# Decode attention and MLP on one core: one loop of eleven rounds, one joining of all heads, w1 in one transfer

## The chip, the core and the metric

The kernel runs on one core of a Trainium2 chip. The metric is device time in microseconds (us); lower is better. Three runs of the kernel before took 675.19, 675.20 and 675.64 us, median 675.2.

## What is computed

Two tokens (batch of 2) go through an attention over a long cache and through a two-layer MLP; a scalar gate mixes the two results. Everything is 32-bit floating point.

```python
g = sigmoid((x * gate_w).sum(-1))                  # x: 2 x 448
q = x @ wq                                         # 16 heads of 256
p = softmax(q . k_cache / 16)                      # k_cache, v_cache: 2 x 16 x 4096 x 256
a = (p . v_cache) @ wo                             # wo: 4096 x 448
b = relu(x @ w1) @ w2                              # w1: 448 x 1792, w2: 1792 x 448
out = g * a + (1 - g) * b
```

The two caches are 268 MB of the 289.5 MB that are read; each element is used once.

## The kernel before

**Units.** One of the 32 pairs of batch and head is a unit. Its keys and values lie in one row of 16384 floats in each of 128 partitions, 8.39 MB, and are brought by one transfer. Three slots in on-chip memory (`slot0` to `slot2`) take turns. Slot 2 holds wq first, and at the end w1 and w2; slot 0 takes wo at the end.

**The engines' parts in a unit.** TensorE (`scores`, L243) makes the scores in the PSUM tile `ps`, four row groups at a time. VectorE (`values`, L268) takes the negative maximum `nm`, ScalarE (`softmax`, L261) the exponential `prob` and its sum `ls`, and then copies the next unit's query (`pick`, L257). VectorE multiplies each of eight stretches of values by `prob` and sums them into `ov` (L274); after the first it signals `room`, which lets TensorE write `ps` again, and after the last it frees the slot. Each of the three engines has a loop of ten rounds of three units (L283) with addresses from a register. The last two units are written out behind the loop (L326).

**Transfers.** SP issues nearly all of them, in order: wq, units 0 and 1, then one unit whenever a slot comes free (L126 to L133), and `late` (L141): when unit 29's slot is free w1, w1x and w2, and when unit 30's is free wo in five pieces (`CUTS`), each with its own semaphore. The last 448 columns of w1 are not in its transfer. They come as w1x: eight transfers of 8 rows each, into partitions 0 to 63:

```python
for k in range(8):
    o = k // 4 * 4 * 8 + k % 4
    e.dma_start(w1x_sb[o:o + 4 * 7 + 1:4], w1x[k]).then_inc(sem["w1x"], 16)
```

**The start.** x and gate_w come by ScalarE's queue. VectorE spreads x (L176, L178), TensorE makes the gate in two forms (L199, L206), then q in two halves with a bank of PSUM each (L217 to L233). The end of q frees slot 2.

**The joining.** A unit's scores were made in four parts with maxima of their own. `combine` (L294) joins them: transposes of `nm` and `ls`, a common maximum, factors `e4`, the weights `wb` (with the gate), their product with the identity, `os` and the products that bring the heads' outputs into the form `ot`. It runs twice, for units 0 to 15 (after the loop, ahead of the last two units) and for units 16 to 31 (at the end, with wo's products in between).

**The end.** TensorE makes w1's products (L343), the hidden layer is transposed, w2's products (L360) go into `acc`, and wo's (`project`, L372) too, for the first 24 of its 32 blocks. The last eight blocks go into `z` in quarters of the columns. `acc` is copied (L391), folded into `z` by four products with `fold` (L394), and the result is copied and stored. The fold stands ahead of the wait for the last pieces of wo:

```python
t = pr.op(dve, lambda e: e.tensor_copy(a_sb, acc), t)
project(n, CUTS[-3])
for g in range(G):
    mm(z[g * R:(g + 1) * R, :DG], flat(fold), a_sb[:, g * DG:(g + 1) * DG], False, False, t, have_fold)
t = project(CUTS[-3], NO)
```

Of the kernel before, what the change touches and what calls it, by code (L numbers as in the profile page):

```python
# [9 lines left out]
G = 4  # L10
R = P // G
SLOTS = 3
NB = 2
ENGINES = ("tensor", "vector", "scalar", "gpsimd", "sync")


class Program:

    def __init__(self, nc):
        self.nc = nc
        self.code = {e: [] for e in ENGINES}
        self.count = dict.fromkeys(ENGINES, 0)

    def op(self, engine, fn, *after):
        self.count[engine] += 1  # L30
        self.code[engine].append(("op", fn, after))
        return engine, self.count[engine]

    def raw(self, engine, fn, *after):
        self.code[engine].append(("raw", fn, after))

    def loop(self, engine, n, fn):
        self.code[engine].append(("loop", n, fn))

    def emit(self, block, sems):  # L40
        def run(name):
            def body(e):
                seen = {}
                for kind, a, b in self.code[name]:
                    if kind == "loop":
                        with e.Fori(0, a) as i:
                            b(e, i)
                        continue
                    for who, n in b:
                        if seen.get(who, 0) < n:  # L50
                            e.wait_ge(sems[who], n)
                            seen[who] = n
                    if kind == "op":
                        a(e).then_inc(sems[name], 1)
                    else:
                        a(e)
            return body

        for name in ENGINES:
            getattr(block, name)(run(name))  # L60
# [7 lines left out]
def gated_mix_decode(nc, xg, kv, wq, w1, w1x, w2, wo, out):  # L68
# [10 lines left out]
    NF = w2.shape[1] // D  # L79
    DG = D // G  # L80
    FG = NF * P // G
    RB = R // B
    HB = H // NB
    UB = U // NB
    HH = HB // G
    CW = 512
    SCALE = float(DH) ** -0.5
    LOOPS = (U - 2) // SLOTS
    assert U == LOOPS * SLOTS + 2 and SLOTS == 3

# [3 lines left out]
    def bank(name, n=CW):  # L94
        return nc.alloc_psum_tensor(name, [P, n], F32).ap()

    NO = NB * HH * J
    CUTS = (0, NO - 18, NO - 8, NO - 4, NO - 1, NO)
    TAIL = 8
    names = [*ENGINES, "xg", "w1x", "w2", *(f"wo{k}" for k in CUTS[1:]), "query", "score", "top", "prob", "room",  # L100
             *(f"land{s}" for s in range(SLOTS)), *(f"free{s}" for s in range(SLOTS)), "out"]
    sem = {n: nc.alloc_semaphore(n) for n in names}
    land = [sem[f"land{s}"] for s in range(SLOTS)]
    free = [sem[f"free{s}"] for s in range(SLOTS)]
    pr = Program(nc)
    pe, dve, act, pool, sp = ENGINES


    sbuf("gap", P, -(-(-nc.sbuf_base // 32) * 32) % 1024 // 4)
    slot = [sbuf(f"slot{s}", P, LEN) for s in range(SLOTS)]  # L110
    ps = bank("ps", SG)
    pw = [bank(f"pw{k}") for k in range(4)]
    acc = bank("acc")[:, :D]


    def load(s, src, signal, lo=0, hi=None):
        hi = src.shape[1] if hi is None else hi
        return lambda e: e.dma_start(slot[s][:, lo:hi], src[:, lo:hi]).then_inc(signal, 16)  # L118

    xg_sb = sbuf("xg_sb", P, KC, B + 1)  # L120
    pr.raw(act, lambda e: e.dma_start(xg_sb, xg).then_inc(sem["xg"], 16))
    pr.raw(sp, load(2, wq, land[2]))
    for u in range(2):
        pr.raw(sp, load(u, kv[u], land[u]))

    def more(e, i):  # L126
        for k in range(SLOTS):
            s = (2 + k) % SLOTS
            take(e, free[s])
            src = kv[bass.ds(i * SLOTS + (2 + k), 1)].rearrange("o p n -> (o p) n")  # L130
            e.dma_start(slot[s], src).then_inc(land[s], 16)

    pr.loop(sp, LOOPS, more)  # L133

    W1, WX = w1.shape[1], w1x.shape[2]
    w1_sb, w1x_sb = slot[2][:, :W1 + WX], slot[2][:, W1:W1 + WX]
    w2_sb = slot[2][:, W1 + WX:W1 + WX + NF * D]

    def late(e):  # L141
        take(e, free[2])
        load(2, w1, land[2])(e)
        for k in range(8):
            o = k // 4 * 4 * 8 + k % 4
            e.dma_start(w1x_sb[o:o + 4 * 7 + 1:4], w1x[k]).then_inc(sem["w1x"], 16)
        e.dma_start(w2_sb, w2).then_inc(sem["w2"], 16)
        take(e, free[0])
        for lo, hi in zip(CUTS, CUTS[1:]):
            load(0, wo, sem[f"wo{hi}"], lo * D, hi * D)(e)  # L150
        take(e, free[1])

    pr.raw(sp, late)

    ident = sbuf("ident", P, P)

    have_ident = pr.op(pool, lambda e: e.memset(ident, 0.0))
    have_ident = pr.op(pool, lambda e: e.affine_select(
        out=ident, in_=ident, compare_op=ALU.not_equal, fill=1.0, base=0, pattern=[[-1, P]], channel_multiplier=1),
        have_ident)  # L160


    sel = sbuf("sel", P, R)
    t = pr.op(dve, lambda e: e.tensor_reduce(sel, ident.rearrange("p (g r) -> p r g", g=G), axis=AX.X, op=ALU.add),
              have_ident)
    fsum = sbuf("fsum", P, B)
    t = pr.op(dve, lambda e: e.tensor_reduce(fsum, sel.rearrange("p (b r) -> p b r", b=B), axis=AX.X, op=ALU.add), t)
    fold = sbuf("fold", P, B, RB)
    have_fold = pr.op(dve, lambda e: e.tensor_scalar(fold, fsum[:, :, None].to_broadcast([P, B, RB]), 1.0 / RB, None,
                                                     op0=ALU.mult), t)  # L170


    xr = sbuf("xr", P, KC, G, B, RB)
    pr.raw(dve, lambda e: e.wait_ge(sem["xg"], 16))
    for g in range(G):
        pr.op(dve, lambda e, g=g: e.tensor_copy(xr[:, :, g], xg_sb[:, :, :B, None].to_broadcast([P, KC, B, RB])))  # L176
    xu = sbuf("xu", P, KC, UB // B, B)
    have_x = pr.op(dve, lambda e: e.tensor_copy(xu, xg_sb[:, :, None, :B].to_broadcast([P, KC, UB // B, B])))  # L178

    def rows_of(c, i=0):  # L180
        return slice(0, P) if c < KF else slice(i * HP, (i + 1) * HP)

    def flat(a):
        return a.rearrange("p b r -> p (b r)")

    def mm(out, lhs, rhs, start, stop, *after):
        return pr.op(pe, lambda e: e.matmul(out, lhs, rhs, start=start, stop=stop), *after)  # L187

    def transpose(out, src, *after):
        return pr.op(pe, lambda e: e.transpose(out, src, ident), *after)  # L190

    def activate(out, src, fn, *after, **kw):
        return pr.op(act, lambda e: e.activation(out, src, fn, **kw), *after)  # L193


    pr.raw(pe, lambda e: e.wait_ge(sem["xg"], 16))
    for c in range(KC):
        r = rows_of(c)
        t = mm(pw[0][:, :1], xr[r, c].rearrange("p g b r -> p (g b r)"), xg_sb[r, c, B:], c == 0, c == KC - 1, have_x)  # L199
    gp = sbuf("gp", P, 1)  # L200
    gate_read = t = activate(gp, pw[0][:, :1], AF.Sigmoid, t)
    omg = sbuf("omg", P, 1)
    have_omg = pr.op(dve, lambda e: e.tensor_scalar(omg, gp, -1.0, 1.0, op0=ALU.mult, op1=ALU.add), t)
    for c in range(KC):
        r = rows_of(c)
        t = mm(pw[1][:UB, :1], xu[r, c].rearrange("p u b -> p (u b)"), xg_sb[r, c, B:], c == 0, c == KC - 1)  # L206
    gu = sbuf("gu", UB, 1)
    have_gu = activate(gu, pw[1][:UB, :1], AF.Sigmoid, t)


    qt = sbuf("qt", P, T, U)
    W = 2 * KF * DH
    WQ = wq.shape[1] // NB
    wide = sbuf("wide", P, CW)
    pr.raw(pe, lambda e: take(e, land[2], 16))
    busy = [(), ()]
    for i in range(NB):  # L217
        w = slot[2][:, i * WQ:(i + 1) * WQ]
        for c in range(KC):
            for g in range(G):  # L220
                r = rows_of(c, g // 2)
                at = g * W + c * CW if c < KF else G * W + g % 2 * CW
                lhs, rhs = flat(xr[r, c, g]), w[r, at:at + CW]
                last = mm(pw[2 + i][g * R:(g + 1) * R, :], lhs, rhs, c == 0, c == KC - 1)
        t = activate(wide, pw[2 + i], AF.Copy, last, *busy[1], scale=SCALE)
        pt = pw[i]
        for k in range(2 * T):
            t2 = transpose(pt[:, k * P:(k + 1) * P], wide[:, k * P:(k + 1) * P], t, gate_read, have_gu)
        busy[1] = (t2,)
        for s in range(2):  # L230
            dst = qt.rearrange("p t (i g s b) -> p i s t g b", i=NB, g=G, s=2)[:, i, s]
            src = pt[:, ::RB].rearrange("p (s t g b) -> p s t g b", s=2, t=T, g=G)[:, s]
            have_q = activate(dst, src, AF.Copy, t2)  # L233

    nm = sbuf("nm", P, U)
    ls = sbuf("ls", P, U)
    ov = sbuf("ov", P, U, J)
    prob = sbuf("prob", P, SG)  # L240
    query = [sbuf(f"query{s}", P, T) for s in range(SLOTS)]

    def scores(e, u, s):  # L243
        take(e, land[s], 16)
# [222 lines left out]
```

## Time and profile before

| | |
|---|---|
| median of three runs | 675.2 us |
| span of the profiled execution (the profile gives no other time of it) | 674.6 us |
| read from HBM | 289.54 MB, 429 GB/s over the span |
| VectorE busy | 341.5 us (51%) |
| TensorE busy | 224.6 us (33%) |
| ScalarE busy | 59.7 us (9%) |
| mean granted TensorE clock | 0.648 of full speed |

The span runs from the first to the last instruction. In the profile PE is TensorE (PEld its weight loads), DVE is VectorE, ACT is ScalarE, POOL is GpSimd and SP is SyncE; a q behind an engine's name stands for its sequencer. A matrix product of 32-bit numbers shows as two instructions. The mean transfer rate holds the start, where nothing has been requested yet, and the end, so it is lower than the rate of the stretch between them. The share of a busy engine does not say whether it sets the time.

### The profile page before, as it was taken

To read this page: it belongs to the slowest core of one execution; us is meant where nothing else is said; L and a number is where in the kernel's file an instruction comes from. 1 tells how busy PE (TensorE), PEld (TensorE's weight loads), DVE (VectorE), ACT (ScalarE), POOL (GpSimd) and SP (SyncE) were. 2 spreads that over 40 slices of the span, in tenths; PEclk is the share of its full clock that TensorE was granted. 3 is DMA by queue.
4 is the path that set the end of the run, shared out by engine and by line. 5 is a ranking of instruction groups with operands and counts; after the bars stand their busy time and mean duration, and the time that the engine had idled before them with its cause. 6 is when DMAs were issued, how large, how long until landed. Compare 5 with 4: busy or idle time off the path is not lost. (4 is left out here: it accounts for less than half of the span.)

```text
span 674.6 us, 4166 instructions
## 1 busy us (share of the span) xinstructions
PE 224.6 (33%) x1323; PEld 67.0 (10%) x1323; DVE 341.5 (51%) x571; ACT 59.7 (9%) x121; POOL 0.7 (0%) x6
## 2 busy tenths in 40 slices
PE   0643221333332123333322333333222333321277
PEld 0210000001001000100100010010001001000022
DVE  0006566544556664455566545455665544657652
ACT  0020001001000100100010010000001001000010
POOL 0000000000000000000000000000000000000000
PEclk9975567667655666765566676665567666556688
DMA  9999999999999999999999999999999999999997
GB/s 381 428 435 436 436 435 435 435 435 435 435 431 435 435 435 435 435 431 435 435 435 435 435 435 435 435 435 435 435 435 435 435 431 427 435 427 435 400 444 316
DMA packets 6180, 289.66 MB, mean 429 GB/s; under 512 B 992, under 2 KB 1120, under 8 KB 1440
## 3 DMA queue, kind: packets, MB, share of 16 engines
q1 hardware_dynamic: 6032, 289.60, 99.3%
q8 instruction: 3, 0.05, 0.0%
q10 hardware_dynamic: 144, 0.01, 0.0%
q14 instruction: 1, 0.01, 0.0%
HBM read 289.54 MB, written 0.06 MB: 429 GB/s over the span
## 5 line engine op out<-in xcount | busy, mean ns | idle before, releaser
L274 DVE SCALAR_TENSOR_TENSOR slot<-slot,prob 128x1024 f32<-128x1024 f32 x256 | 295.9, 1222 | 65.1 <-DVEq L65 65.1
L251 PE MATMUL ps<-slot,query 128*32 128x512 f32 x1024 | 190.8, 909 | 404.4 <-PEq L65 404.3
L270 DVE TENSOR_REDUCE nm<-ps 128x1024 f32 (+1 forms) x32 | 39.2, 1225 | 230.8 <-DVEq L65 230.8
L251 PEld LDWEIGHTS ps<-slot,query 128*32 128x32 f32 x1024 | 54.7, 158 | 539.1 <-issue 539.0
L263 ACT ACTIVATE prob<-ps,nm 128x1024 f32<-128x1024 f32 x32 | 35.6, 1113 | 385.0 <-ACTq L65 384.9
L263 ACT ACT_TABLE_LOAD x10 | 12.8, 1283 | 163.4 <-ACTq L65 163.4
L274 DVE DVE_READ_ACCUMULATOR slot<-slot,prob (+1 forms) x256 | 21.3, 83 | 0.0
L187 PE MATMUL pw<-slot,xr 128*32 128x512 f32 (+3 forms) x96 | 12.9, 671 | 1.3 <-DMA slot<-in_w1x 1.3
L176 DVE COPY xr<-xg_sb 128x128 f32<-128x128 f32 x4 | 0.6, 224 | 18.0 <-DMA xg_sb<-in_xg 18.0
L187 PE MATMUL pw<-xg_sb,xr 128*128 128x1 f32 (+1 forms) x8 | 1.9, 352 | 21.2 <-DVE xu L178 21.2
L187 PE MATMUL acc<-slot,ot 128*32 128x448 f32 x48 | 7.2, 661 | 2.3 <-DMA slot<-in_wo 2.2
L258 ACT ACTIVATE query<-qt 128x2 f32 (+1 forms) x32 | 6.2, 193 | 0.0
L263 ACT ACTIVATION_READ_ACCUMULATOR prob<-ps,nm (+1 forms) x32 | 6.2, 193 | 0.0
L187 PE MATMUL acc<-slot,hr 128*32 128x448 f32 x28 | 4.9, 810 | 2.0 <-DMA slot<-in_w 2.0
L190 PE MATMUL pw<-ident,nm 128*16 128x128 f32 x2 | 0.7, 328 | 12.6 <-DVEq L324 12.6
L187 PEld LDWEIGHTS pw<-xg_sb,xr 128*128 128x128 f32 (+1 forms) x8 | 1.8, 321 | 21.2 <-DMA xg_sb<-in_xg 21.2
L187 PEld LDWEIGHTS pw<-slot,xr 128*32 128x32 f32 (+1 forms) x96 | 2.8, 122 | 9.9 <-issue 7.7
L190 PE MATMUL pw<-ident,wide 128*128 128x128 f32 x11 | 1.9, 288 | 2.4 <-ACT wide L193 2.4
L310 DVE TENSOR_TENSOR os<-ov,pw 128x128 f32<-128x128 f32 x2 | 0.6, 287 | 4.0 <-PE pw L187 4.0
L318 DVE COPY ot<-pw 128x256 f32<-128x256 f32 x4 | 1.5, 420 | 2.0 <-PE pw L187 2.0
L391 DVE COPY wide<-acc 128x448 f32<-128x448 f32 x1 | 0.6, 624 | 3.1 <-PE pw L187 3.1
L187 PE MATMUL pw<-slot,ot 128*32 128x112 f32 x64 | 2.0, 261 | 0.2 <-DMA slot<-in_wo 0.2
(42 smaller groups left out, 20.9 us busy)
## 6 DMA issues: line engine op xcount, KB each, us to landing
slot<-in_wq SPq DMA_DIRECT2D x1, 7168.0 KB, 19.4
slot<-in_w SPq DMA_DIRECT2D x1, 3136.0 KB, 29.9
slot<-in_wo SPq DMA_DIRECT2D x1, 3136.0 KB, 21.2
slot<-in_w SPq DMA_DIRECT2D x1, 2912.0 KB, 28.2
slot<-in_wo SPq DMA_DIRECT2D x1, 2240.0 KB, 26.1
slot<-in_wo SPq DMA_DIRECT2D x1, 896.0 KB, 27.8
slot<-in_wo SPq DMA_DIRECT2D x1, 672.0 KB, 28.9
slot<-in_kv SPq DMA_DIRECT2D x32, 38.4
```

The costliest lines, as they stand in the source:

```text
L176: pr.op(dve, lambda e, g=g: e.tensor_copy(xr[:, :, g], xg_sb[:, :, :B, None].to_broadcast([P, KC, B, RB])))
L187: return pr.op(pe, lambda e: e.matmul(out, lhs, rhs, start=start, stop=stop), *after)
L190: return pr.op(pe, lambda e: e.transpose(out, src, ident), *after)
L251: m = e.matmul(ps[g * R:(g + 1) * R, c * CW:(c + 1) * CW], query[s][:, t:t + 1].to_broadcast([P, R]), slot[s][:, lo:lo + CW], start=(t == ...
L258: e.activation(query[s], qt[:, :, bass.ds(u, 1)].rearrange("p t o -> p (t o)"), AF.Copy).then_inc(sem["query"], 1)
L263: e.activation(prob, ps, AF.Exp, bias=nm[:, bass.ds(u, 1)], accum_out=ls[:, bass.ds(u, 1)]).then_inc(sem["prob"], 1)
L270: e.tensor_reduce(nm[:, bass.ds(u, 1)], ps, axis=AX.X, op=ALU.max, negate=True).then_inc(sem["top"], 1)
L274: m = e.scalar_tensor_tensor(v, v, 1.0, prob, op0=ALU.mult, op1=ALU.mult, accum_out=ov[:, bass.ds(u, 1), j])
L310: t = pr.op(dve, lambda e: e.tensor_tensor(os, ov[:, us], wp[:, :UB, None].to_broadcast([P, UB, J]), op=ALU.mult), t)
L318: t = pr.op(dve, lambda e, hh=hh: e.tensor_copy(ot[:, i, hh], po[:, hh * B * J:(hh + 1) * B * J].rearrange("p (b j o) -> p j b o", j=J, o= ...
L391: t = pr.op(dve, lambda e: e.tensor_copy(a_sb, acc), t)
```

## The change

The kernel is written anew, with a function for each engine in place of lists of operations. What it computes and the number of bytes stay as they are. The parts:

- **Loop.** TensorE runs all 32 units in one loop of eleven rounds; the third unit of a round stands under a branch that the last round does not take. VectorE's loop runs by unit, and the slot's address comes from a register (`u % SLOTS`). ScalarE keeps ten rounds and two units behind them. There is one `query` buffer instead of three, one semaphore `free` for all slots, and no `room`.
- **Joining.** One joining of all 32 units after the last unit's scores. Its steps for VectorE stand under branches inside the last unit's multiplies (after the fourth and the seventh). The gate is applied where `lhs` (before: `ot`) is written.
- **Last unit.** Its keys and its values come by two transfers, with a semaphore of their own for the values (`late`).
- **w1** comes by one transfer of 128 rows; w1x is gone.
- **wo** comes in six pieces of 14, 6, 4, 4, 3 and 1 blocks; before, five of 14, 10, 4, 3 and 1.
- **Start.** The gate is made from sums by GpSimd and one product; `ident` is made after x has landed; both halves of q use one bank; 1 - g is multiplied into x for the MLP (`xo`) in place of the hidden layer.
- **End.** Waits are instructions of their own that count the semaphore down again (`take`). The four products with `fold` stand behind the wait for the piece of three blocks.

```diff
+    def sync(e):
+        bring(e, slab(2, 0, NQ * WQ), wq, sem["wq"])
+        for u in range(2):
+            bring(e, slot[u], kv[u], land[u])
+        with e.Fori(0, U // SLOTS) as i:
+            for k in range(SLOTS):
+                take(e, sem["free"])
+                s = (k + 2) % SLOTS
+                src = kv[bass.ds(i * SLOTS + (k + 2), 1)].rearrange("o p n -> (o p) n")
+                if k < SLOTS - 1:
+                    bring(e, slot[s], src, land[s])
+                    continue
+                with e.If(i == U // SLOTS - 1):
+                    bring(e, slot[s][:, :T * S], src[:, :T * S], land[s])
+                    bring(e, slot[s][:, T * S:], src[:, T * S:], sem["late"])
+                with e.Else():
+                    bring(e, slot[s], src, land[s])
+        take(e, sem["free"])
+        bring(e, slab(2, 0, W2), w1, sem["w1"])
+        bring(e, slab(2, W2, W2 + NF * D), w2, sem["w2"])
+        take(e, sem["free"])
+        for lo, hi in zip(WO, WO[1:]):
+            bring(e, slab(0, (lo - NF) * D, (hi - NF) * D), wo[:, (lo - NF) * D:(hi - NF) * D], sem[f"wo{hi}"])
...
+    def tensor(e):
...
+        with e.Fori(0, -(-U // SLOTS)) as i:
+            for s in range(SLOTS - 1):
+                scores(s)
+            with e.If(i < U // SLOTS):
+                scores(SLOTS - 1)
+        take(e, sem["query"])
+        e.transpose(tp[:U, :P], nm, ident)
+        e.transpose(tp[:U, P:2 * P], ls, ident).then_inc(sem["tr"], 1)
+        take(e, sem["xo"])
+        take(e, sem["w1"], 16)
+        project(xo, FG, lambda c, g: (g % 2 * W1 + (g // 2 * KF + c if c < KF else 2 * KF) * FG, g // 2))
...
+        for k in range(N - DIRECT, N):
+            if k in WO:
+                e.wait_ge(sem[f"wo{WO[WO.index(k) + 1]}"], 16)
+            if k == N - 4:
+                take(e, sem["a"])
+                for g in range(G):
+                    e.matmul(z[g * R:(g + 1) * R], fold.rearrange("p b r -> p (b r)"), a_sb[:, g * DG:(g + 1) * DG],
+                             start=False, stop=False)
+            for g in range(G):
+                m = e.matmul(z[g * R:(g + 1) * R], lhs[:, k], slab(0, (k - NF) * D + g * DG, (k - NF) * D + (g + 1) * DG),
+                             start=k == N - DIRECT, stop=k == N - 1)
...
+    def vector(e):
...
+        with e.Fori(0, U) as u:
+            take(e, sem["score"], G)
+            e.tensor_reduce(nm[:, bass.ds(u, 1)], ps, axis=AX.X, op=ALU.max, negate=True).then_inc(sem["top"], 1)
+            take(e, sem["prob"])
+            with e.If(u == U - 1):
+                e.wait_ge(sem["late"], 16)
+            for j in range(J):
+                v = ring[:, bass.ds((u % SLOTS) * LEN + (T * S + j * SG), SG)]
+                m = e.scalar_tensor_tensor(v, v, 1.0, prob, op0=ALU.mult, op1=ALU.mult,
+                                           accum_out=ov[:, bass.ds(u, 1), j])
+                if j == 3:
+                    with e.If(u == U - 1):
+                        take(e, sem["tr"])
+                        e.tensor_reduce(nb, mt, axis=AX.X, op=ALU.min).then_inc(sem["nb"], 1)
+                if j == 6:
+                    with e.If(u == U - 1):
+                        take(e, sem["e4"])
...
+            m.then_inc(sem["free"], 1)
```

## Rows read from the trace of the kernel before

**Rows 1.** The page, 40 slices of the span: rate in each, and the bytes.
```profile
GB/s 381 428 435 436 436 435 435 435 435 435 435 431 435 435 435 435 435 431 435 435 435 435 435 435 435 435 435 435 435 435 435 435 431 427 435 427 435 400 444 316
HBM read 289.54 MB, written 0.06 MB: 429 GB/s over the span
```

**Rows 2.** The chain of waits in order of time: start us, us, what.
```profile
642.65 28.93 DMA slot<-in_wo
...
671.63 1.10 PE pw L187 x32
...
672.75 0.27 DVE res L397
```

**Rows 3.** Waits of SP's queue: us in total, times, longest.
```profile
SPq L65 <- SPq L65: 630.0, 34, 33.7
```

**Rows 4.** Transfers by line: count, KB each, median us to landing.
```profile
slot<-in_kv SPq DMA_DIRECT2D x32, 38.4
slot<-in_w1x SPq DMA_DIRECT2D x8, 28.0 KB
```

**Rows 5.** Stretches: us, busy PE, PEld, DVE, ACT, POOL, clock, DMA share, GB/s.
```profile
174.40:232.35 57.95, 17.83 (x96) 5.14 (x96) 31.17 (x52) 5.18 (x10) 0.00 (x0) 0.62 0.99 423
...
580.05:638.00 57.95, 18.93 (x108) 5.12 (x108) 32.34 (x60) 4.15 (x10) 0.00 (x0) 0.62 1.00 435
```

**Rows 6.** Timeline of unit 29: start us, us, engine, line, operation.
```profile
601.80 4.91 PE L251 MATMUL ps<-slot,query 128*32 128x512 f32 x32 [13.28 <-PEq L65]
...
607.06 1.23 DVE L270 TENSOR_REDUCE nm<-ps 128x1024 f32 x1 [6.07 <-DVEq L65]
...
619.28 0.34 SPq L118 DMA_DIRECT2D slot<-in_w  x1
...
619.67 5.48 SPq L146 DMA_DIRECT2D slot<-in_w1x  x8
```

**Rows 7.** Timeline of the start: x there, slot 2 free, unit 1's scores.
```profile
20.34 0.63 DVE L176 COPY xr<-xg_sb 128x128 f32<-128x128 f32 x4 [18.04 <-DMA xg_sb<-in_xg]
...
36.19 0.35 SPq L131 DMA_DIRECT2D slot<-in_kv  x1
...
59.21 6.54 PE L251 MATMUL ps<-slot,query 128*32 128x512 f32 x32 [13.35 <-PEq L65]
```

**Rows 8.** Sequencer instructions of L274, L46, L65: ns min/median/max.
```profile
L274 DVEq FUSED_REGOPS  x240: 57/57/57, 50.3 to 611.2; - x120
...
L46 DVEq COMPARE_BRANCH  x10: 50/56/67, 92.0 to 612.4; - x10
...
L65 PEldq EVENT_SEMAPHORE  x99: 51/51/51, 21.3 to 655.2; - x99
```

**Rows 9.** The page, instruction queue: packets, MB, share of 16 engines.
```profile
q8 instruction: 3, 0.05, 0.0%
```

**Rows 10.** Stretches at the end, columns as in rows 5.
```profile
670.00:670.50 0.50, 0.50 (x21) 0.50 (x23) 0.13 (x1) 0.00 (x0) 0.00 (x0) 1.00 0.62 251
670.50:671.00 0.50, 0.50 (x22) 0.32 (x14) 0.49 (x1) 0.00 (x0) 0.00 (x0) 1.00 0.64 247
671.00:671.50 0.50, 0.44 (x10) 0.16 (x8) 0.00 (x0) 0.00 (x0) 0.00 (x0) 1.00 0.22 82
671.50:672.00 0.50, 0.37 (x16) 0.37 (x20) 0.00 (x0) 0.00 (x0) 0.00 (x0) 1.00 0.04 14
```

**Rows 11.** Timeline of TensorE at the end: w1, w2, wo, fold.
```profile
648.07 3.35 PE L187 MATMUL pw<-slot,xr 128*32 128x448 f32 x32 [1.29 <-DMA slot<-in_w1x]
...
655.12 4.90 PE L187 MATMUL acc<-slot,hr 128*32 128x448 f32 x28 [1.96 <-DMA slot<-in_w]
...
662.53 1.72 PE L187 MATMUL acc<-slot,ot 128*32 128x448 f32 x8 [2.19 <-DMA slot<-in_wo]
...
666.10 4.19 PE L187 MATMUL acc<-slot,ot 128*32 128x448 f32 x32
...
671.04 0.40 PE L187 MATMUL pw<-wide,fold 128*32 128x112 f32 x8
```

More of the change, by code (lines that the diff above doesn't have):

```diff
@@ L12 @@
 SLOTS = 3
[L13 to L60, printed above, removed]
+CW = 512
+DIRECT = 8
 def take(e, sem, n=1):
@@ L65, in take, with settle, gated_mix_decode @@
     e.sem_inc(sem, -n)
-def gated_mix_decode(nc, xg, kv, wq, w1, w1x, w2, wo, out):
+def settle(e, sem, op):
+    op.then_inc(sem, 1)
+    take(e, sem)
+def gated_mix_decode(nc, xg, kv, wq, w1, w2, wo, out):
     U, _, LEN = kv.shape
@@ L95, in bank @@
         return nc.alloc_psum_tensor(name, [P, n], F32).ap()
[L97 to L101, printed above, removed]
+    WO = [NF]
+    for n in (14, 6, 4, 4, 3, 1):
+        WO.append(WO[-1] + n)
+    assert WO[-1] == N
+    names = ["xg", "wq", "w1", "w2", *(f"wo{k}" for k in WO[1:]), *(f"land{s}" for s in range(SLOTS)), "late",
+             "pool", "vec", "act", "const", "fold", "sums", "gate", "omg", "xo", "proj", "wide", "pt", "hr",
+             "query", "score", "top", "prob", "free", "tr", "nb", "e4", "wb", "wp", "os", "po", "ot",
+             "acc", "a", "z", "res", "out"]
@@ L120, in gated_mix_decode @@
-    xg_sb = sbuf("xg_sb", P, KC, B + 1)
[L121 to L133, printed above, removed]
@@ L137, in gated_mix_decode @@
[L137 to L151, printed above, removed]
@@ L153, in gated_mix_decode @@
-    pr.raw(sp, late)
+    ring = sbuf("ring", P, SLOTS * LEN)
+    slot = [ring[:, s * LEN:(s + 1) * LEN] for s in range(SLOTS)]
+    xg_sb = sbuf("xg_sb", P, KC, B + 1)
     ident = sbuf("ident", P, P)
[L157 to L160, printed above, removed]
+    ones = sbuf("ones", P, P)
     sel = sbuf("sel", P, R)
-    t = pr.op(dve, lambda e: e.tensor_reduce(sel, ident.rearrange("p (g r) -> p r g", g=G), axis=AX.X, op=ALU.add),
-              have_ident)
@@ L177, in gated_mix_decode @@
[L177 to L213, printed above, removed]
-    wide = sbuf("wide", P, CW)
[L215 to L233, printed above, removed]
@@ L239, in gated_mix_decode @@
     ov = sbuf("ov", P, U, J)
[L240 to L244, printed above, removed]
-        take(e, sem["query"])
-        take(e, sem["room"])
-        for c in range(SG // CW):
-            for t in range(T):
-                for g in range(G):
-                    lo = t * S + g * SG + c * CW
-                    m = e.matmul(ps[g * R:(g + 1) * R, c * CW:(c + 1) * CW],
-                                 query[s][:, t:t + 1].to_broadcast([P, R]), slot[s][:, lo:lo + CW],
-                                 start=(t == 0), stop=(t == T - 1))
-                    if c == SG // CW - 1 and t == T - 1:
-                        m.then_inc(sem["score"], 1)
@@ L323, in gated_mix_decode @@
-    have_ot = []
-    for _ in combine(0, pr.op(dve, lambda e: e.drain())):
-        pass
-    for u in range(LOOPS * SLOTS, U):
-        for e, f in stages.items():
-            more = (u + 1 < U,) if e == act else ()
-            pr.raw(e, lambda e_, f=f, u=u, more=more: f(e_, u, u % SLOTS, *more))
-    done = pr.op(dve, lambda e: e.drain())
-    hs = wide[:, :FG]
-    hr = sbuf("hr", P, NF, R)
-    ph, pt = pw[3], pw[2]
-    pr.raw(pe, lambda e: (take(e, land[2], 16), e.wait_ge(sem["w1x"], 16 * 8)))
@@ new lines, in gated_mix_decode, with slab @@
+    wb = sbuf("wb", U, G, R)
+    os = sbuf("os", P, U, J)
+    lhs = sbuf("lhs", P, N, R)
+    a_sb = wide[:, :D]
+    res = sbuf("res", P, DG)
+    ps = bank("ps", SG)
+    ph, pt, po, tp = (bank(n) for n in ("ph", "pt", "po", "tp"))
+    acc = bank("acc")[:, :D]
+    z = bank("z")[:, :DG]
+    mt, lt, wp, gp = tp[:U, 0:P:R], tp[:U, P:2 * P:R], tp[:, 2 * P:2 * P + U], tp[:, 3 * P:3 * P + B]
+    W2 = 2 * W1
+    def slab(s, lo, hi, rows=slice(0, P)):
+        return ring[rows, s * LEN + lo:s * LEN + hi]
```

324 lines of the change are left out of this document (171 added, 153 removed).

## The prediction

> **What bounds the kernel now.** I read the page's transfer rate first. Apart from the first slice and the last three the queues move 427 to 436 GB/s in every slice, and 289.54 MB at 435 GB/s are 665.6 us of the span's 674.6 [rows 1]. The chain of waits says the same of the end: its last 33 us are 28.9 us of landing wo, then 1.1 us of TensorE and 0.27 us of VectorE [rows 2]; the store closes the span. The third view is the waits of SP, which issues nearly all transfers: 34 waits, 630.0 us together, all for a slot to come free [rows 3]. That looks like a queue kept waiting, and is not: a unit's transfer lands 38.4 us after its issue [rows 4], while 8.39 MB at 434 GB/s take 19.3 us, so at every issue another unit's 19 us are still ahead. The transfers are the bound; an engine counts only before the first transfer, after the last, or where it delays an issue by more than 19 us.
>
> The profile gives no other time of its execution than the span, 674.6 us. The median of the three runs is 675.2, so I put 0.6 us around the span and carry it through. About 0.2% (1.35 us) is what a measurement of this kernel can tell from no change.
>
> **The change part by part.**
>
> *The loop of eleven rounds, VectorE by unit, branches.* Unit 29 shows the period: scores at 601.80, maximum at 607.06, slot free before 619.28 [rows 6]. VectorE is taken for 12.2 us of 19.3, so 7 us a unit are spare, and 19 us of latency before the queue would run dry. The new loop adds register operations for the slot's address and three branches a unit. One register operation took 57 ns and one branch 56 ns, and both ran under the multiplies of 1.22 us [rows 8]. From nothing (all hidden) up to three operations for each of 8 multiplies and three branches, all exposed: 8 x 3 x 0.057 + 3 x 0.056 = 1.5 us. Both ends lie inside the 7 us: I take 0. The one `query` buffer and the dropped `room` add no wait: the next query is written after the exponential has read `ps`. SP's new branch costs 0.05 to 0.1 us ahead of an issue with 19 us of cover: 0.
>
> *The start.* The gate now goes through GpSimd, `ident` is made after x has landed, and the two halves of q share one bank, so they run strictly in turn. x is there at 20.34, slot 2 is free at 36.19, and unit 1 is there at 59.21 [rows 7]. Slot 2's next load has to be issued before about 58. From x to the free slot it is 16 us now; GpSimd's steps and the serial halves add between 0 and half of that again, 8 us; cover 22 us, taken as 0. Unit 0's scores may start about 1 us later, which 19 us of cover hide too.
>
> *One joining of all heads.* The first half's joining stood between units 29 and 30 and delayed only unit 30; it goes, for nothing, because wo, which waits for that slot, is queued about 14 us (w1 and w2) ahead of its turn. The last unit's keys now land 9.6 us before its values, so its maximum and exponential are done when the values land. From about 641: eight multiplies 9.2 us, up to 2 us for the pieces in between, then the joining's last steps, 3 us: about 655. wo's first piece is waited for until 662.53 [rows 11]. So it is hidden, with 7 us of cover.
>
> *w1 in one transfer of 128 rows.* Its issue falls from nine transfers to one, 5.5 us of SP [rows 6]. That was hidden, since unit 31 was still coming: 0. What counts is where the bytes go. w1x moves 8 x 28.0 KB [rows 4] in transfers of 8 rows; the others have 128. The engines do not end together: the share of the 16 that is busy is 0.62 from 670.0, 0.64 from 670.5, 0.22 from 671.0 and 0.04 from 671.5 [rows 10]. That is about six done at 670, eight more by 671, and two or three late until 671.6, the landing that the chain ends with [rows 2]. One engine moves 434/16 = 27.1 GB/s; 229 KB over eight engines are 1.06 us each, just the step between the six and the eight. I read the eight as w1x's engines, and the late ones as two of the other eight. Spread over sixteen, w1x's share is 0.53 us for each: the eight end 0.53 us sooner, the late ones 0.53 us later. If the late ones are of the eight it is -0.53. I take +0.53, since otherwise the middle step would not hold eight.
>
> [...]
>
> *The order at the end.* Before, the four folding products (eight instructions, 0.40 us) ran at 671.04, ahead of the wait for wo's next to last piece [rows 11]; the last 32 instructions then took 1.10 us from its landing [rows 2]. In the new code the wait comes first and the products stand behind it, with the last four k's queued behind them. At 1.10/32 = 0.034 us each, eight are 0.27 us; the bounds are 0.27 and the whole 0.40. I take 0.27. The waits are instructions of their own now; one took 51 ns on TensorE [rows 8]; two on the path, 0.1 us, between 0 and 0.2. The cut of wo into six pieces and of unit 31 into two adds no bytes; I put it at 0, within 0.1 either way.
>
> *Code.* Three instruction fetches of 0.05 MB in all ran beside the transfers [rows 9]: 16 KB at 27.1 GB/s is 0.6 us of one engine, and whoever serves it stays behind. With two units' scores no longer unrolled, one fetch can go, or move to another engine. Bounds -0.6 and +0.6; I take -0.1.
>
> Sum: 0.53 + 0.27 + 0.1 - 0.1 = +0.8 us. Span 675.4, time **676.0 us**. Bounds: -0.53 + 0.27 + 0 - 0.6 - 0.1 = -1.0 and 0.53 + 0.40 + 0.2 + 0.6 + 0.1 = +1.8.
>
> **The rivals.**
>
> *The balance goes the other way, or the late engines are gone.* Then -0.53 or less replaces +0.53: 675.2 - 0.53 + 0.27 + 0.1 - 0.1 = 674.9. For it: the windows name no engine. Against it: the step of eight.
>
> *TensorE falls behind at the end (slower).* Before, unit 31's scores ended shortly before w1's products, which took 3.35 us for 32 at full clock [rows 11]. Now TensorE idles about ten us before them, and work after an idle stretch starts at the low clock: unit 1's 32 took 6.54 us [rows 7]. w1 would end 3 us later, w2 about 662 instead of 660. From wo's first piece 48 instructions remain up to the copy of `acc`: at the fast 4.19/32 = 0.131 us they are 6.3 us, at the slow 1.72/8 = 0.215 us 10.3 us [rows 11]. Add 1.1 us for the next four k's. From 662.5 that is 669.9 or 673.9, and the landing that matters is about 672.1. It decides once TensorE needs over 9.6 us here, that is if it stays slow for nearly all 48; the price is then 1.8 us and about 1 us for the last 40 instructions: 678.8. Against it: before, the slow stretch lasted 3 us and the 32 that followed were fast.
>
> *Branches bring code in again.* Ten rounds' backward branches cost no fetch before: three in the whole span [rows 9]. Were each of eleven rounds to fetch 16 KB on one engine, 11 x 0.6 = 6.6 us: 682. [...]
>
> *The queue loses less (faster).* The stretch 174 to 232 moved 423 GB/s where the last full one moved 435 [rows 5]: 1.6 us. Did that not recur, with 674.9 besides, 673.3. Nothing in the change touches it, as far as I see.
>
> **How the numbers follow.** Forecast 0.70 (676.0, its own range 675.2 to 676.9); balance the other way 0.13 (674.9); TensorE behind 0.09 (678.8); code fetched again 0.03 (682); queue loses less 0.05 (673.3). The range 674.6 to 677.2 takes in the first two with nearly all bounds and leaves out the rest, 0.17. Slower by over 0.2% is above 676.55: a fifth of the forecast, 0.14, with 0.12 of the slow rivals: 0.26. Faster, below 673.85: 0.05. Within: 0.69.
>
> **What would show it.** The share of busy engines in the last 3 us should fall in one large step and leave two or three late ones, later by 0.5 us than before; a last landing earlier than before's refutes the w1 term. The eight folding instructions should stand behind the wait for wo's next to last piece, with about 1.4 us from there to the end of TensorE. Unit transfers should still be 38 us from issue to landing; much less means that the queue ran dry and the first part is wrong. More instruction packets than the three would speak for the code rival; a granted clock near 0.5 from 663 to 669, with the copy of `acc` after the last landing, for TensorE.

## The result and the profile after

The changed kernel takes 676.68 us (median of 21 runs, 676.33 to 678.21) beside 675.64 us (21 runs, 675.19 to 676.71) for the kernel before: a ratio of 1.0014, 95% interval 1.0008 to 1.0021, so 0.5 to 1.4 us longer. The forecast was 676.0 us and +0.8 us. The profiled execution has a span of 675.3 us, 0.7 more than before's.

The page after, in the lines that answer to [rows 1], [rows 4] and [rows 9] (the last two from its list of transfers and of DMA queues):

```profile
GB/s 381 427 436 435 435 435 435 435 435 435 435 435 435 435 435 435 435 435 435 435 435 435 435 435 435 435 435 435 435 435 435 435 435 435 435 435 425 426 434 282
...
q8 instruction: 3, 0.05, 0.0%
...
HBM read 289.54 MB, written 0.06 MB: 429 GB/s over the span
...
ring<-in_kv SPq DMA_DIRECT2D x31, 38.7
```

The transfers still set the pace: the same bytes, 435 GB/s in the middle, 38.7 us from a unit's issue to its landing. Three instruction packets of 16 KB and one of 8 KB, as before. What differs is the end. The stretches of 57.95 us and of the last microseconds after (us; busy PE, PEld, DVE, ACT, POOL; clock; DMA share; GB/s), to be held against [rows 5] and [rows 10]:

```profile
174.40:232.35 57.95, 17.36 (x96) 4.39 (x96) 31.40 (x52) 5.18 (x10) 0.00 (x0) 0.65 1.00 434
...
669.50:670.00 0.50, 0.34 (x16) 0.35 (x20) 0.36 (x1) 0.00 (x0) 0.00 (x0) 1.00 0.57 219
670.00:670.50 0.50, 0.50 (x28) 0.39 (x17) 0.26 (x1) 0.00 (x0) 0.00 (x0) 1.00 0.16 65
670.50:671.00 0.50, 0.13 (x8) 0.00 (x0) 0.00 (x0) 0.00 (x0) 0.00 (x0) 1.00 0.11 43
671.00:671.50 0.50, 0.15 (x8) 0.18 (x12) 0.00 (x0) 0.00 (x0) 0.00 (x0) 1.00 0.07 25
671.50:672.00 0.50, 0.50 (x28) 0.50 (x25) 0.00 (x0) 0.00 (x0) 0.00 (x0) 1.00 0.00 0
```

The first row is the stretch whose rate I had put down as a rival: before's profile shows 423 GB/s there, this one 434. I had read too much into it. These views count a packet whole where it starts. A unit's packets are 65.5 KB, and 16 of them are under way at once (at 100, 300 and 500 us of both traces), so about 1 MB can fall to either side of an edge, which is 18 GB/s over 57.95 us. In the last full stretch, 580.05 to 638.00, it is the other way round: 435 before [rows 5], 425 after. Over all the full stretches together both profiles moved the same (before, then after):

```profile
58.50:638.00 579.50, 180.54 (x972) 52.49 (x972) 314.09 (x515) 50.72 (x100) 0.00 (x0) 0.62 1.00 433
```

```profile
58.50:638.00 579.50, 178.04 (x992) 44.91 (x992) 314.98 (x513) 50.49 (x99) 0.00 (x0) 0.64 1.00 433
```

With each packet of the trace shared out over its own time, before is 0.32 MB behind after from 232 us on, which is 0.7 us and not 1.6. A later kernel (eight drains, further down) is as far behind from 290 us on. So executions differ by this much on the way, and two profiles can't be subtracted as they are. The other rows show the new shape of the end: where before had two steps (0.62 and 0.64, then 0.22), the share falls from 0.57 to 0.16 at once. After's trace has 16 increments of a semaphore for the landing of wo's next to last piece: 14 of them come by 670.03 us, and two late ones at 670.78 and 671.21.

The end itself, timeline after (start us, us, engine, line, operation), beside [rows 11] and [rows 2]:

```profile
646.99 4.95 PE L174 MATMUL ph<-ring,xo 128*32 128x448 f32 x32 [5.69 <-PEq L19]
...
655.02 3.20 PE L230 MATMUL acc<-ring,lhs 128*32 128x448 f32 x28
...
662.21 7.24 PE L230 MATMUL acc<-ring,lhs 128*32 128x448 f32 x48 [3.98 <-DMA ring<-in_wo]
...
671.35 0.40 PE L238 MATMUL z<-wide,fold 128*32 128x112 f32 x8 [0.72 <-PEq L19]
671.54 0.97 PE L241 MATMUL z<-ring,lhs 128*32 128x112 f32 x32
673.09 0.28 DVE L326 COPY res<-z 128x112 f32<-128x112 f32 x1 [2.83 <-DVEq L19]
673.39 0.35 SPq L111 DMA_DIRECT2D out<-res  x1
```

w2's products are over at 658.2, wo's first piece is waited for (idle 3.98 us), so the joining is hidden. The folding products now start behind the landing. And the last product ends at 671.54 + 0.97 = 672.51, but the copy starts at 673.09: 0.58 us. Before's timeline has the same 32 products from 671.63, for 0.97 as well, to 672.60, and the copy at 672.75: 0.15 us.

```profile
671.63 0.97 PE L187 MATMUL pw<-slot,ot 128*32 128x112 f32 x32 [0.19 <-DMA slot<-in_wo]
672.75 0.27 DVE L397 COPY res<-pw 128x112 f32<-128x112 f32 x1 [1.76 <-PE pw L187]
```

The chain of waits puts 0.48 us of after's down to "issue", that is to no wait that the profile knows, where before's has 0.02 between its two pieces ([rows 2]: 671.63 + 1.10 = 672.73 to 672.75):

```profile
672.60 0.48 issue
673.09 0.28 DVE res L326
```

Nothing in my sum had half a microsecond there.

### The profile page after: what moved, and what is told of

Read it like the earlier page. It is cut to its first block, busy times and chain, and to the rows that moved or that the text cites. A ratio compares the mean times of both kernels' runs of the same rounds, so it can differ in the third digit from the quotient of the medians.

```text
span 675.3 us, 4348 instructions
## 1 busy us (share of the span) xinstructions
PE 214.3 (32%) x1297; PEld 56.7 (8%) x1297; DVE 339.1 (50%) x556; ACT 59.2 (9%) x119; POOL 2.2 (0%) x14
## 5 line engine op out<-in xcount | busy, mean ns | idle before, releaser
L301 DVE SCALAR_TENSOR_TENSOR ring<-ring,prob 128x1024 f32 x256 | 296.0, 1221 | 77.3 <-DVEq L19 77.3
L189 PE MATMUL ps<-ring,query 128*32 128x512 f32 x1024 | 183.0, 880 | 415.1 <-PEq L19 415.1
L295 DVE TENSOR_REDUCE nm<-ps 128x1024 f32 x32 | 39.2, 1225 | 213.9 <-DVEq L19 213.9
L189 PEld LDWEIGHTS ps<-ring,query 128*32 128x32 f32 x1024 | 46.2, 154 | 551.2 <-issue 551.2
L301 DVE DVE_READ_ACCUMULATOR ring<-ring,prob x256 | 21.2, 83 | 0.0
L230 PE MATMUL acc<-ring,lhs 128*32 128x448 f32 x76 | 10.4, 688 | 4.0 <-DMA ring<-in_wo 4.0
L174 PE MATMUL ph<-ring,xr 128*32 128x512 f32 (+1 forms) x64 | 9.9, 759 | 1.7 <-PEq L19 1.7
L174 PE MATMUL ph<-ring,xo 128*32 128x448 f32 (+1 forms) x32 | 5.0, 766 | 5.7 <-PEq L19 5.7
L230 PEld LDWEIGHTS acc<-ring,lhs 128*32 128x32 f32 x76 | 3.0, 134 | 10.8 <-issue 5.9
L174 PEld LDWEIGHTS ph<-ring,xr 128*32 128x32 f32 (+1 forms) x64 | 2.1, 129 | 7.9 <-issue 7.9
## 6 DMA issues: line engine op xcount, KB each, us to landing
ring<-in_kv SPq DMA_DIRECT2D x2, 4096.0 KB, 33.9
ring<-in_kv SPq DMA_DIRECT2D x31, 38.7
```

What stands on the lines that cost most here:

```text
L174: m = e.matmul(ph[g * R:(g + 1) * R, :width], x[r, c], slab(2, at, at + width, r), start=c == 0, stop=c == KC - 1)
L189: m = e.matmul(ps[g * R:(g + 1) * R, c * CW:(c + 1) * CW], query[:, t:t + 1].to_broadcast([P, R]), slot[s][:, at:at + CW], start=t == 0, s ...
L230: m = e.matmul(acc[g * R:(g + 1) * R], lhs[:, k], w, start=k < G, stop=k >= N - DIRECT - G)
L295: e.tensor_reduce(nm[:, bass.ds(u, 1)], ps, axis=AX.X, op=ALU.max, negate=True).then_inc(sem["top"], 1)
L301: m = e.scalar_tensor_tensor(v, v, 1.0, prob, op0=ALU.mult, op1=ALU.mult, accum_out=ov[:, bass.ds(u, 1), j])
```

## The experiments

My theory: the change costs what the last microseconds cost, by terms that add (w1's balance, the order of the folding products, the last wait). The rivals: the terms are not what holds the end (TensorE, VectorE or the joining is), or the half microsecond is something else than the wait. The interval of one comparison is about 0.6 us to either side, so a single term of 0.3 to 0.5 us is read from the trace, and the times judge the sums.

Beside the times I give the median span of all executions of a kernel (21 of the changed kernel: 675.3 us; 11 or 12 of each variant; 101 of the kernel before beside the experiments: 674.3). The two can disagree, because a time is longer than its span: by 1.3 to 1.45 us in the executions of the two kernels, but by 1.7 to 2.0 us in some of the variants of the changed one (six of 11 with the last wait in the copy, nine of 11 with three parts taken back, two of 11 with two). In the three profiled executions among these the trace has an 8 KB instruction packet 1.6 to 1.7 us behind the span's end; no other profile has one there.

**w1 whole in the kernel before.**

```diff
-        for k in range(8):
-            o = k // 4 * 4 * 8 + k % 4
-            e.dma_start(w1x_sb[o:o + 4 * 7 + 1:4], w1x[k]).then_inc(sem["w1x"], 16)
...
```

(Left out: w1's one transfer takes in these columns, and TensorE's wait for `w1x` goes.)

> The kernel before with only w1 changed to one transfer of 128 rows. My theory (w1x's eight transfers kept eight engines 1.06 us busier, and the late ones are two of the other eight): the middle step in the share of busy engines goes, most end together near the old mean, the late ones end about 0.5 us later; time of before plus 0.5 us. Rival 1 (the late ones are of w1x's eight): minus 0.5 us. Rival 2 (split or whole is all the same): 0, and the middle step stays.

675.65 us, ratio to before 0.9998 (0.9989 to 1.0007). The stretches at the end:

```profile
670.00:670.50 0.50, 0.50 (x24) 0.50 (x20) 0.12 (x1) 0.00 (x0) 0.00 (x0) 1.00 0.25 100
670.50:671.00 0.50, 0.50 (x20) 0.33 (x10) 0.50 (x1) 0.00 (x0) 0.00 (x0) 1.00 0.17 68
671.00:671.50 0.50, 0.50 (x14) 0.22 (x16) 0.00 (x1) 0.00 (x0) 0.00 (x0) 1.00 0.13 50
```

The middle step is gone, as the theory has it, and shares of 0.25 to 0.13 are left, two to four of the 16 engines. That these end 0.5 us later was not seen: the last products start at 671.44 here, at 671.63 in before's profile.

```profile
671.44 0.97 PE L184 MATMUL pw<-slot,ot 128*32 128x112 f32 x32
```

Nor does the time show it: its interval, -0.7 to +0.5 us, holds 0 and ends just short of 0.53, and the median span is before's, 674.3 us.

**w1x back in the changed kernel.**

```diff
-        bring(e, slab(2, 0, W2), w1, sem["w1"])
+        bring(e, slab(2, 0, W2 - WX), w1, sem["w1"])
+        for k in range(8):
+            o = k // 4 * 4 * 8 + k % 4
+            bring(e, slab(2, W2 - WX, W2, slice(o, o + 4 * 7 + 1, 4)), w1x[k], sem["w1x"])
...
```

(Left out: TensorE's wait for `w1x` and the addresses of its columns.)

> The changed kernel with w1x's eight transfers put back, nothing else. My theory: six engines end first, eight about 1 us later, the late ones about 0.5 us earlier than without w1x; the whole 0.5 us shorter than the changed kernel, so about 0.5 us above before. Rival 1: 0.5 us longer than the changed kernel. Rival 2: the same as the changed kernel.

676.82 us, ratio 1.0018 (1.0009 to 1.0027). In the profiled execution the folding products start at 670.81 instead of 671.35, and its span is 674.6 us instead of 675.3.

```profile
670.81 0.40 PE L243 MATMUL z<-wide,fold 128*32 128x112 f32 x8 [0.72 <-PEq L19]
```

But this is the shortest of the 11 executions; their median span is 675.4, no shorter than the changed kernel's. So the run fits my theory in its trace, and the second rival in its times and spans; more on this further down.

**Folding products ahead of the wait.** (The same two statements, `if k == N - 4` before `if k in WO`.)

> The changed kernel with the four folding products ahead of the wait for wo's next to last piece. My theory: from that piece's landing to the last product 1.1 us instead of 1.4, the whole 0.27 us shorter than the changed kernel. Rival (TensorE is not what the last copy waits for, or the copy of acc comes late): 0, with the folding products still after the landing.

676.65 us, ratio 1.0008 (0.9999 to 1.0017), span of the profiled execution 675.3, median 675.0. The timeline:

```profile
670.71 0.38 PE L236 MATMUL z<-wide,fold 128*32 128x112 f32 x8
671.50 0.97 PE L241 MATMUL z<-ring,lhs 128*32 128x112 f32 x32 [0.41 <-DMA ring<-in_wo]
673.06 0.27 DVE L326 COPY res<-z 128x112 f32<-128x112 f32 x1 [3.53 <-DVEq L19]
```

The products moved ahead of the landing, and from the landing to the last product it is 0.97 us now, while after's products from 671.35 to 672.51 take 1.16 and themselves begin behind the landing: about 0.2 us. But in this execution the landing came 0.15 us later, and the 0.6 us ahead of the copy stayed. The time alone can't show the term; the median span is 0.3 us below the changed kernel's.

**The last wait carried by the copy.**

```diff
-        take(e, sem["z"])
+        e.wait_ge(sem["z"], 1)
         e.tensor_copy(res, z).then_inc(sem["res"], 1)
```

> The changed kernel with VectorE's last wait (for z) carried by the copy itself instead of an instruction that also counts the semaphore down. In the changed kernel 0.5 us passed between that wait's end and the copy, 0.1 us in other places with the same pair. Theory A (the pair of instructions costs it): the copy starts within 0.1 us of the last product, 0.4 us shorter. Theory B (something else holds VectorE at this point, as the code fetch that starts at the same time): the gap stays, within 0.1 us the same.

676.26 us, ratio 1.0007 (0.9998 to 1.0016), span of the profiled execution 674.8, median 674.7:

```profile
671.59 0.98 PE L241 MATMUL z<-ring,lhs 128*32 128x112 f32 x32
672.62 0.27 DVE L326 COPY res<-z 128x112 f32<-128x112 f32 x1 [2.50 <-PE z L241]
```

From the last product (672.57) to the copy 0.05 us instead of 0.58, 0.4 us less in time and 0.6 us less in the median span. It speaks for the pair of instructions; the next three took that apart.

**The wait apart, in the kernel before.**

```diff
-    t = project(CUTS[-3], NO)
+    t0 = project(CUTS[-3], NO)
     res = sbuf("res", P, DG)
-    t = pr.op(dve, lambda e: e.tensor_copy(res, z[:, :DG]), t)
+    pr.raw(dve, lambda e: (e.wait_ge(sem[pe], t0[1]), e.sem_inc(sem["room"], 1)))
+    t = pr.op(dve, lambda e: e.tensor_copy(res, z[:, :DG]))
```

> The kernel before with VectorE's last wait (ahead of the copy of the result) as an instruction of its own. Theory A (an instruction apart costs 0.5 us at this place): the copy starts 0.5 us after the last product and the time of before rises by 0.45 us. Theory B (it costs 0.1 us as elsewhere, and the gap of the changed kernel has to do with its code): 0.1 us.

675.70 us, ratio 1.0004 (0.9995 to 1.0013). The timeline at its end:

```profile
670.92 0.97 PE L187 MATMUL pw<-slot,ot 128*32 128x112 f32 x32
672.15 0.28 DVE L398 COPY res<-pw 128x112 f32<-128x112 f32 x1 [1.82 <-PE pw L187]
```

The last product ends at 671.89, the copy starts at 672.15: 0.26 us, 0.1 more than before's 0.15. A wait apart costs 0.1 us here, not 0.5, so the pair of instructions alone isn't the cause. (The wait's instruction counts another semaphore up here, not its own down; the next run has the very pair.)

**Eight drains at the head of VectorE's program** (`for _ in range(8): e.drain()`), the wait left as it is in the changed kernel.

> The changed kernel with eight drain instructions at the head of VectorE's program, where it waits anyway; the last wait stays an instruction of its own. Theory A (the 0.5 us between that wait and the last copy come from where the copy stands in VectorE's code): the copy starts 0.1 us after the wait, 0.4 us shorter than the changed kernel, about 676.3. Theory B (the pair of instructions costs 0.5 us here wherever it stands; the four reductions of the other run did something else): the gap stays at 0.5.

676.30 us, ratio 1.0007 (0.9998 to 1.0016). First the end of this run's timeline, then that of the changed kernel with 16 unused products on TensorE (two experiments on), which left VectorE's program alone:

```profile
672.18 0.98 PE L241 MATMUL z<-ring,lhs 128*32 128x112 f32 x32
673.33 0.28 DVE L328 COPY res<-z 128x112 f32<-128x112 f32 x1 [1.99 <-DVEq L19]
```

```profile
671.87 0.97 PE L243 MATMUL z<-ring,lhs 128*32 128x112 f32 x32
673.42 0.28 DVE L328 COPY res<-z 128x112 f32<-128x112 f32 x1 [2.47 <-DVEq L19]
```

673.16 to 673.33 is 0.17 us, 672.84 to 673.42 is 0.58. The same pair of instructions costs 0.1 or 0.5 us according to where it stands in VectorE's program.

The sequencer's rows of the traces, which the timeline leaves out, show what the place does. From the end of the wait to the copy 0.49 us pass in the changed kernel and in the three variants with the gap, 0.09 in the three without. Those 0.40 us have not gone in the run with eight drains. They stand eight VectorE instructions earlier, between the last multiply's read of the accumulator and the next wait, where 0.55 us pass instead of 0.14. With the last unit in one transfer, which makes VectorE's program shorter, they stand two instructions later, behind the copy and its drain (0.46 us instead of 0.05). So in these kernels VectorE's sequencer stops once for 0.40 us at one place of its code, and this shows ahead of the last copy only where that place lies behind the last wait. The reason stays open. What the traces show beside it is an instruction packet of 8 KB: it starts 1.1 to 1.2 us after the stop begins in the five kernels that have the stop in the last 3 us (after: 672.60 and 673.76). That the two belong together is not shown. With the wait carried by the copy no stop is seen behind the last product.

**Four more reductions a unit on VectorE.**

```diff
                 if j == 3:
+                    with e.If(u < U - 1):
+                        for x in range(4):
+                            e.tensor_reduce(extra[:, bass.ds(u, 1), x], prob, axis=AX.X, op=ALU.max)
```

> The changed kernel with four reductions of 128x1024 more on VectorE in each unit but the last (results unused), about 4.5 us of 19.3 more. My theory (7 us a unit are spare, the transfers set the pace): the same time within 0.2 us, units still 38 us from issue to landing. Rival (VectorE's unit is near the pace): each unit is longer by what passes 19.3 us; 1 us a unit would be 30 us in all.

676.49 us, ratio 1.0012 (1.0003 to 1.0021), 0.2 below the changed kernel. Groups of instructions (count, busy us, mean ns) and the unit's transfer:

```profile
L307 DVE TENSOR_REDUCE extra<-prob 128x1024 f32 x124 | 142.4, 1210 | 0.0
...
L296 DVE TENSOR_REDUCE nm<-ps 128x1024 f32 x32 | 39.2, 1224 | 79.0 <-DVEq L19 79.0
```

```profile
ring<-in_kv SPq DMA_DIRECT2D x31, 33.9
```

142 us more of VectorE, none of it in the time. Slots come free later, so a transfer is issued 4.8 us later and waits that much less in the queue: 33.9 us to landing instead of 38.7, still far over one unit's 19.3. (The shift of VectorE's program also closed the half microsecond at the end: the copy starts at 672.82, 0.17 us after the last product. The 0.2 us less in time are no gain of the reductions.)

**16 unused products on TensorE** ahead of w1's.

```diff
+        for _ in range(16):
+            e.matmul(z, ident, ones[:, :DG], start=True, stop=True)
         take(e, sem["xo"])
```

> The changed kernel with 16 unused products on TensorE between the last unit's transposes and w1's products, so that it doesn't idle there. My theory (the low clock of w1's products is hidden by the wait for w2 and wo): w1's 32 instructions take about 3.4 us instead of 4.95, the granted clock in that stretch is 1.0, and the time is the same within 0.2 us. Rival (TensorE behind sets the end): shorter by what w1's products gain, 1 us or more.

676.88 us, ratio 1.0017 (1.0008 to 1.0026).

```profile
641.76 5.04 PE L209 MATMUL z<-ones,ident 128*128 128x112 f32 x32
...
647.27 3.35 PE L174 MATMUL ph<-ring,xo 128*32 128x448 f32 x32 [0.47 <-PEq L19]
...
662.53 7.60 PE L232 MATMUL acc<-ring,lhs 128*32 128x448 f32 x48 [3.00 <-DMA ring<-in_wo]
```

w1's products fell from 4.95 us, after 5.69 us of idling and at a mean granted clock of 0.67, to 3.35 us, which is what the kernel before took for them at a granted clock of 1.00. The time didn't fall: the gain goes into the wait for wo. TensorE doesn't set the end here.

**The last unit in one transfer** (the branch in SP's loop and the wait for `late` taken out).

> The changed kernel with the last unit's keys and values in one transfer. My theory (the joining is hidden by 7 us now; without the split the last unit's chain starts 9.7 us later, less about 2 us of maximum and exponential that ran behind unit 30): ot about 661, wo's products start about 1 to 2 us late, time 0 to 0.5 us longer. Rival 1 (all heads' joining is hidden anyhow): 0, wo's first products still wait for their transfer. Rival 2 (the joining sets the end as soon as the split goes): 2 us or more longer.

676.70 us, ratio 1.0010 (1.0001 to 1.0019).

```profile
658.75 0.38 PE L208 MATMUL tp<-ident,wb 32*128 32x32 f32 x2 [2.46 <-PEq L19]
...
660.98 9.89 PE L223 MATMUL acc<-ring,lhs 128*32 128x448 f32 x74
...
671.40 0.62 DVE L315 COPY wide<-acc 128x448 f32<-128x448 f32 x1 [8.88 <-DVEq L19]
672.12 0.40 PE L231 MATMUL z<-wide,fold 128*32 128x112 f32 x8
672.31 0.98 PE L234 MATMUL z<-ring,lhs 128*32 128x112 f32 x32
```

wo's products now trail: `acc` is copied at 671.40 instead of 669.64, and the folding products wait for it until 672.12 (after: 671.35). That is 0.8 us later. VectorE's program got shorter by the wait and a branch, the half microsecond before the last copy went (673.29 to 673.46), and so the time is level with the changed kernel and 0.4 us above the one with the shifted program, the fair partner (in median spans 675.3 and 674.9). So the joining of all heads is hidden only because of the split; with it TensorE still waits 3.98 us for wo's first piece.

**Parts taken back together.** The folding products and the last wait (two), and w1x as well (three):

> The changed kernel with the folding products ahead of the wait and the last wait carried by the copy, w1 still in one transfer. My theory (the terms add): 0.27 and 0.45 us below the changed kernel, about 676.0, and 0.3 to 0.5 us above the kernel that has w1x's eight transfers as well (675.67). Rival (w1's transfer costs nothing in time): level with that kernel and with before.

> The changed kernel with three parts taken back at once: w1x's eight transfers, the folding products ahead of the wait, the last wait carried by the copy. My theory: the terms add, -0.5 (last landing), -0.27 (products) and -0.45 (copy) against the changed kernel: span 674.1, time 675.5 us, level with before. Rival (the lost time lies elsewhere, as in the code fetch beside the store or in what follows the span): at most half of it comes back, 676.1 or more.

Two: 675.84 us, ratio 1.0002 (0.9993 to 1.0011), span of the profiled execution 674.3, median 674.4. Three: 675.67 us, ratio 1.0001 (0.9992 to 1.0010), span 673.8, median 674.0. Ends of their chains of waits, two first:

```profile
671.35 1.02 PE z L241 x32
672.36 0.02 issue
672.39 0.27 DVE res L326
```

```profile
670.79 1.02 PE z L246 x32
671.81 0.02 issue
671.83 0.28 DVE res L331
```

Both are level with before, so the order of the products and the wait are most of what the change cost, by the medians 0.84 us (676.68 to 675.84) of 1.04. This is clear of the noise: the 11 executions with two parts lie between 675.33 and 676.44 us, the changed kernel's 21 between 676.33 and 678.21.

The two kernels differ in w1x alone, and in both the last products wait for wo's next to last piece: it is there 0.56 us earlier with w1x. The other profiles bear this out, the one with the last unit in one transfer left out, where the folding products wait for `acc`. The products behind that piece start at 670.79 to 671.63 us in the five profiles with w1x (median 670.92) and at 671.35 to 671.99 in the eight without (median 671.46): 0.54 us. That is the size and the sign of my term in the landing.

Between the times of the two kernels it is 0.17 us, between their median spans 0.4, and with w1x back in the changed kernel, or w1 whole in the one before, it is nothing. The spans say why that can be. Of before's 101, 55 lie at 673.8 to 674.4 us, 40 at 674.9 to 676.2 and 6 between; with w1 whole all 11 lie between 674.0 and 674.9. So w1x seems to end the transfers earlier in some executions and later in others, as it would if the late engines were sometimes of the eight that I read as its own and sometimes not, the two cases of my forecast. The traces name no engine, and none of the five with w1x is from the upper end of its kernel's spans, so this isn't shown.

**64 drains at the head of TensorE's program**, on the kernel with three parts taken back.

> As the kernel with three parts taken back, and 64 drain instructions at the head of TensorE's program, where it waits for x anyway. Theory A (TensorE's code is fetched in blocks ahead of need, and the third block's fetch falls into the end because of where the code stands): all fetches come 64 instructions earlier, the last one at or before 667 instead of 672, and the store's last landing follows its issue by 1.55 us instead of 1.85; 0.3 us shorter than without the drains. Theory B (the fetch has nothing to do with TensorE's place in its code): fetches and store as without the drains.

675.60 us, ratio 1.0003 (0.9994 to 1.0012), span 674.1. Store: 1.6 us from issue to landing with and without the drains, so the 0.3 us to be gained wasn't there. In the changed kernel it took 1.9:

```profile
out<-res SPq DMA_DIRECT2D x1, 56.0 KB, 1.9
```

Across the kernels it is 1.6 to 1.9 us, with and without instruction packets in the stretch ahead of it. What makes the difference I couldn't settle. Of the three 16 KB packets the middle one came 9 us earlier with the drains (650.88 instead of 659.84 us) and the others did not (43.73 and 670.86 instead of 43.67 and 670.71), so neither theory holds as it stands.

## Why the prediction was right, point by point

- **The bound, and that nothing on the way counts.** Right. 142 us more of VectorE cost nothing, the start hides in its cover (slot 2's next load was issued at 37.47 us instead of 36.19), and w1's products are hidden at a granted clock of 0.67.
- **w1 in one transfer, +0.53 us.** Right in the traces: the step comes and goes with w1x (shares of 0.62 and 0.64 before, 0.55 and 0.54 with three parts taken back), and the products behind the landing that counts start 0.54 us later without it, between the medians of the profiles. Of that landing's 16 increments five come by 669.76 us before, eight from 670.64 to 670.97 and three from 671.30 to 671.59; after, thirteen come from 669.31 to 669.72. That the eight are w1x's engines was my reading; no trace names an engine. The last of these increments came 0.4 us earlier after than before, which I had named as a refutation. By this single pair the term failed. The test was too weak for it: before's profile was 0.7 us behind on the way, and its landing is the latest of the five with w1x. In the times the term isn't shown: 0.17 us between the pair, nothing in the other two comparisons.
- **Folding products, +0.27 us.** Their place behind the landing and about 0.2 us show in the trace, 0.3 us in the median spans. In the times it shows only together with the wait (from 676.26 to 675.84 us).
- **Waits as instructions of their own, +0.1 us within 0 to 0.2.** This term was mis-sized. One of them cost 0.5 us at the end of VectorE's program, because the stop of 0.40 us fell just behind it; carried by the copy it is gone from the trace, and the time is 0.4 us shorter (less than one comparison can tell by itself). Elsewhere it is the 0.1 that I had taken.
- **Code, -0.1 us.** As many packets as before; no gain. A 16 KB packet took 0.95 to 0.97 us in the profiles before and after, not the 0.6 of my sum. That whoever serves it stays behind was an estimate, and no trace names the engine. The landings fit it: in the profile after, one of the 16 increments of the last unit's values comes 0.8 us behind the other fifteen (639.44 and 638.63 us) after one such packet, and two of wo's come late after two. The store took up to 0.3 us longer, from a cause that stays open, and that wasn't in the sum.
- **The joining, 7 us of cover.** Hidden, w2's products over 4 us before wo arrives. The heads' outputs are written by 656.4 us, about 655 in the forecast. The cover hangs on the split of the last unit, as worked out.
- **The rivals.** TensorE behind: it idled 5.69 us ahead of w1's products, not ten; they took 4.95 us, not 6.4, and w2's were over at 658.2, not 662. Code fetched again: three packets. The queue losing less: its 1.6 us came from the edges of a stretch, as shown above; the real difference between the two profiles is 0.7 us, and one of the later kernels shows it too.

The sign was right and the size within the range, but the sum came out so near in part by luck. Two thirds of the forecast 0.8 us were w1's term, which the times don't show. Most of the measured 1.04 us, 0.84, is the order of the products and the last wait, for which I had taken 0.37; in the median spans the wait is 0.6 of these 0.9 us, and I had taken it for 0.1.

## What to carry to other kernels

When the transfers fill the time, as here, where 142 us more of VectorE cost nothing, a rewrite is worth what it does in the few microseconds after the last landing: keep everything that can run earlier ahead of the last waits in an engine's order, and let the last waits be carried by the instructions that need them. In the profiles with w1x's transfers of 8 rows the products behind the landing that counts start half a microsecond earlier (0.54 us between the medians); the times don't show it. So the share of busy engines in the last microseconds is worth a view of its own. Don't subtract two profiles before the long middle stretch has been compared, don't read a rate off a stretch that is short for the packets in it, and look at the spans of all executions, not only of the profiled one.

## What had not been expected of the hardware

- The same wait and copy on VectorE took 0.1 us or 0.5 us from the wait's end to the copy, according to where they stood in its program. A stop of 0.40 us moved with the code: eight instructions earlier with eight drains at the head, two later in a program made shorter.
- The store of 56 KB took 1.6 to 1.9 us from issue to landing in kernels that issue it alike.
- Executions of the kernel before fall into two groups of spans, about 1 us apart (55 and 40 of 101); those of the kernel with w1 whole don't.
